# A fused recurrence and maxout MoE on one core: another order of the first loads and of the steps

## The chip, the cores and the metric

The kernel runs on one core of a Trainium2 chip. A core has five engines that work side by side, each through its own queue and in order: TensorE (PE, with its weight loads listed as PEld), VectorE (DVE), ScalarE (ACT), GpSimd (POOL) and SyncE (SP), which here issues all the DMA transfers. An instruction that waits holds up everything behind it on its engine. The metric is the time of one execution in microseconds (us).

## The reference

Two steps follow one another. The first is a gated linear recurrence over time for 4 batches of 8 heads with 768 steps and head size 48; the second takes its outputs, laid out as 3072 tokens of 384 numbers, through a feed-forward layer that keeps the larger of two projections.

```python
for t in range(S):
    state = alpha[:, :, t, :, None] * state + np.einsum('bhd,bhe->bhde', k[:, :, t], v[:, :, t])
    y[:, :, t] = np.einsum('bhd,bhde->bhe', q[:, :, t], state)
...
h1 = x @ w1
h2 = x @ w2
g = np.maximum(h1, h2)
return (g @ w_out)
```

All inputs and the output are float32.

## The kernel before

The work is cut into 12 units (u = 0 to 11). Unit u is a stretch of 256 time steps of one batch: the batch is u mod 4 and the stretch is u div 4, so that units 0 to 3 begin the four batches and unit u takes its state from unit u − 4. A unit has two chunks (cc) of 128 steps.

The recurrence of a unit is done in chunks. `ln` takes the logarithm of alpha on ACT (tile lg). `sums` makes running sums of it on PE with constant masks (tile cs, and the chunk decays dps in a corner of the first cs). `expm`, `expp` and `expd` make exp(−cs) in Em, exp(cs) in place, and the decays de, all on ACT. `kmul` forms kn = k·Em on POOL, `qmul` forms qn = q·exp(cs) on VectorE. `turn` transposes both on PE (tile tp) and copies them out on VectorE (qk). `kvmm` multiplies kn by v for the state, `kvsum` takes that out of PSUM on VectorE (tm) and `state` scales it on POOL (sb). `pmm` forms the products of k and q on PE (pp) and `pmask` masks them on VectorE (pt). `ystate` and `yin` add up the output y from the state and from the masked products (ya), and ACT casts it (xn). `xturn` transposes it (xp), and VectorE copies that to xt, the input of the MoE.

The MoE uses max(h1, h2) = relu(h1 − h2) + h2. So it needs w1 − w2 (`wsub`, VectorE, in four quarters, tile w12), and w2·w_out (tile w2o), which PE forms once: `wturn` transposes w2, `wcast` casts w_out to 16 bits in two halves on ACT and POOL, `wmul` multiplies in two halves, `wout` copies the result out on ACT. `hid(u, f2)` makes one of four hidden pairs, six matmuls and a ReLU (on ACT, or on VectorE for the fourth pair unless told otherwise; tile gT). `outp(u, n)` makes one of the two output blocks: three matmuls of xt with w2o, eight of gT with w_out; ACT copies the block to outs and SP stores it. `vcast` casts v on POOL and ACT. `dummies` issues matmuls on zeros (tile warm) whose results nobody reads.

PSUM has eight banks. They are handed out under three tags: "m" with two banks in turn (hidden pairs, outputs, w2 transposes, dummies), "pp" with two (the products; in the beginning two parts of w2·w_out), and "g" with four in turn (cs, tp, kv, ya, xp, and one part of w2·w_out).

The order on every engine is the order in which the program calls these steps (a manual schedule, lines 465 to 617): a hand-written start for units 0 to 2, then a loop in which iteration u does the state and the y of unit u, the sums, exponentials and turns of unit u + 1, and the MoE of unit u − 1. The loads have four buffers for each input; iteration u issues the loads of unit u + 4. The loads before the loop stand on SP in the order of lines 113 to 122: all of unit 0, w2, w_out, w1, all of unit 1.

Of the kernel before, what the change touches and what calls it, by code (L numbers as in the profile page):

```python
# [15 lines left out]
def kernel(  # L16
# [27 lines left out]
    nc = tc.nc  # L44
# [162 lines left out]

    def sums(u):
        X = st[u]
        lg = X["lg"]  # L210
        cs = [new("g", [128, 512], FP32, 4, "cs") for _ in range(2)]
        X["csv"] = csv = [x[:, 0 : H * D].rearrange("p (h d) -> p h d", h=H) for x in cs]
        X["dps"] = dps = cs[0][:, H * D : H * D + 4 * HP].rearrange("p (j b n) -> p j b n", j=HP, b=2)
        for hp in range(HP):
            for j in range(2):
                nc.tensor.matmul(
                    dps[:, hp], lhsT=pair(lg[:, j], hp), rhs=halves, start=(j == 0), stop=(j == 1)
                )
        for j in range(2):
# [159 lines left out]
    def xturn(u):  # L379
        X = st[u]  # L380
        xp = new("g", [128, ND, 2, C], FP16, 4, "xp")
        for cc in range(2):
# [24 lines left out]

    def outp(u, n):
        X = st[u]
        d, b = divmod(u, B)  # L410
        if n == 0:
            X["outs"] = mp.tile([128, 2, DM], FP32, tag="outs", bufs=2, name="outs")
        op = new("m", [128, DM], FP32, 2, "op")
        for ds in range(ND):
            nc.tensor.matmul(op, lhsT=X["xt"][:, ds, n, :], rhs=w2o[:, ds, :], start=(ds == 0), stop=False)  # L415
        for f in range(NF):
# [19 lines left out]
    def wmul(n):  # L436

        if n == 0:
            wqs.extend([new("pp", [128, DM], FP32, 2, "wq") for _ in range(2)] + [new("g", [128, DM], FP32, 4, "wq")])
        for ds in range(ND):  # L440
# [54 lines left out]
    kvsum(0, 1)  # L495
    ystate(0)
    dummies(2)
    wturn(1)
    yin(0)
    wturn(2)  # L500
    wcast(0)
    dummies(2)
    xturn(0)
    ln(1)
    dummies(4)
    wmul(0)
    wcast(1)
    wsub(0)
    wsub(1)
    wsub(2)  # L510
    wsub(3)
    wmul(1)
    sums(1)
    wout()

    load(3)
    hid(0, 0, False)
    expm(1, 0)
    expp(1, 0)
    hid(0, 1, True)  # L520
    kmul(1, 0)
    qmul(1, 0)
    expm(1, 1)
    expp(1, 1)
    hid(0, 2, False)
    expd(1)
    kmul(1, 1)
    qmul(1, 1)
    vcast(1)
    hid(0, 3, True)  # L530
    load(4)
    turn(1, 0)
    turn(1, 1)
    outp(0, 0)
    kvmm(1, 0)
    pmm(1, 0)
    kvmm(1, 1)
    kvsum(1, 0)
    state(1, 1)
    pmask(1, 0)  # L540
    kvsum(1, 1)
    ln(2)
    dummies(3)
    pmm(1, 1)
    pmask(1, 1)
    ystate(1)
    outp(0, 1)
    yin(1)
    sums(2)
    exps(2)  # L550
    dummies(3)
    xturn(1)
    for cc in range(2):
        kmul(2, cc)
    state(2, 0)
    vcast(2)
    for cc in range(2):
        qmul(2, cc)
    dummies(2)
    hid(1, 0)  # L560
    hid(1, 1)
    turn(2, 0)
    hid(1, 2)
    turn(2, 1)
    hid(1, 3)
    load(5)


    for u in range(2, NU):
# [8 lines left out]
        if more(u):  # L578
            kvmm(u, 1)
        if nxt:  # L580
            ln(u + 1)
        if u > 2:
            hid(u - 1, 0)
            hid(u - 1, 1)
        else:
            outp(1, 0)
        if nxt:
# [10 lines left out]
        if u > 2:  # L598
            hid(u - 1, 2)
            hid(u - 1, 3)  # L600
        if nxt:
            for cc in range(2):
                qmul(u + 1, cc)
        yin(u)
# [42 lines left out]
```

## Time and profile before

| what | value |
|---|---|
| median of 11 runs | 157.35 us (156.52 to 158.69) |
| the profiled execution's own time | 156.48 us |
| its span, first to last instruction | 154.8 us |
| mean granted TensorE clock | 0.978 |
| PE busy | 140.4 us, 91% |
| VectorE busy | 93.8 us, 61% |
| ACT busy | 91.4 us, 59% |
| POOL busy | 56.3 us, 36% |
| read from and written to HBM | 23.59 MB and 4.72 MB |

The profile is one execution. Busy time is the time in which an engine ran an instruction; a wait is idle time and is put down to the event that ended it. The dummies count as busy (35 of them, 11.8 us), so a busy PE is not always useful. A stage view gives the busy times in a stretch of the span and the share of its clock that PE was granted there. The chain of waits is followed back from the last instruction. A DMA row gives the issue on SP; its landing comes later by the time that the DMA view lists.

### The profile page before, as it was taken

The page shows a single profiled execution, that of the slowest core. Times are in us where ns is not written, and L with a number is a line of the kernel's source. Part 1 is how long each engine was busy: PE and PEld are TensorE (multiplying, and loading weights), DVE is VectorE, ACT ScalarE, POOL GpSimd, SP SyncE. Part 2 cuts the span into 40 slices and gives each one's busy share as a digit, 9 for nine tenths or more (in the row PEclk, how much of TensorE's full clock was granted, in tenths as well). Part 3 has the DMA queues.
Part 4 walks back from the last instruction along what each step waited for, and adds up shares of the span by engine and source line. Part 5 has one row for each costly group of instructions (what it writes and reads, how often), then busy time and mean ns, then how long its engine had stood idle before and what let it go on. Part 6 is the DMA issues. An engine that isn't in the chain of part 4 may idle for free.

```text
span 154.8 us, 4245 instructions
## 1 busy us (share of the span) xinstructions
PE 140.4 (91%) x1683; PEld 101.5 (66%) x1683; DVE 93.8 (61%) x191; ACT 91.4 (59%) x188; POOL 56.3 (36%) x111
## 2 busy tenths in 40 slices
PE   6965993998999898999999999999999999999991
PEld 2334751574677586777787777887778778767760
DVE  5058772085558778676687784957757577664110
ACT  3475405473393778486694884966938579445421
POOL 7391400064081626219055171371632805410000
PEclk9999699599999999999999999999999999999999
DMA  4999999999699897988969899797896902020202
GB/s 121 267 388 374 357 300 238 204 171 227 108 246 139 226 229 128 235 131 235 204 115 309 121 248 209 128 319 111 197 263 113 309 16 89 4 102 4 95 6 102
DMA packets 76339, 28.58 MB, mean 185 GB/s; under 512 B 71712, under 2 KB 74528, under 8 KB 76320
## 3 DMA queue, kind: packets, MB, share of 16 engines
q1 hardware_dynamic: 76320, 28.32, 79.3%
q8 instruction: 13, 0.21, 0.7%
q14 instruction: 6, 0.05, 0.1%
HBM read 23.59 MB, written 4.72 MB: 183 GB/s over the span
## 4 chain that ended last, share of the span: by engine, by line
PE 68%; SPq 8%; DMA 7%; DVE 6%; ACT 5%; issue 4%; POOL 1%; ACTq 0%; DVEq 0%
PE op L417 20%; PE hp L399 16%; PE op L415 8%; DMA af<-in_alpha_dram 7%; PE tp L285 6%; SPq L121 4%; PE pp L334 3%; PE cs L226 3%; DVE pt L340 3%; SPq L75 2%; PE xp L386 2%; PE wq L442 2%; PE ya L370 2%; PE kv L307 2%; ACT cs L241 2%
## 5 line engine op out<-in xcount | busy, mean ns | idle before, releaser
L274 POOL TENSOR_TENSOR kn<-kf,Em 128x384 f16<-128x384 f32 x24 | 23.5, 997 | 35.2 <-ACT Em L236 35.2
L399 PE MATMUL hp<-xt,w 128*128 128x256 f16 x288 | 35.8, 273 | 0.3 <-DVE xt L388 0.2
L417 PE MATMUL op<-wo,gT 128*128 128x384 f16 x192 | 35.1, 326 | 0.0
L340 DVE TENSOR_TENSOR pt<-pp,um 128x512 f16<-128x512 f32 x48 | 30.9, 686 | 3.1 <-PE pp L334 2.4
L420 ACT COPY outs<-op 128x384 f32<-128x384 f32 x24 | 11.5, 478 | 35.4 <-PE op L417 24.3
L399 PEld LDWEIGHTS <-w 128*128 128x128 f16 x288 | 26.8, 98 | 5.2 <-issue 1.3
L417 PEld LDWEIGHTS <-gT 128*128 128x128 f16 x192 | 18.8, 98 | 12.4
L266 POOL TENSOR_TENSOR sb<-tm,dd 128x192 f16<-128x192 f32 x20 | 10.1, 506 | 42.4 <-DVE tm L320 31.2
L404 ACT ACTIVATE gT<-hp 128x512 f16<-128x512 f32 x35 | 20.8, 598 | 4.9 <-PE hp L399 3.9
L292 DVE COPY qk<-tp 128x1024 f16<-128x1024 f16 x20 | 13.7, 687 | 11.6 <-PE tp L285 11.6
L406 DVE TENSOR_SCALAR gT<-hp 128x512 f16<-128x512 f32 x13 | 9.0, 692 | 15.4 <-PE hp L399 15.4
L320 DVE TENSOR_TENSOR tm<-kv,sb 64x192 f32<-64x192 f32 x32 | 11.3, 352 | 8.7 <-PE kv L307 8.4
L415 PE MATMUL op<-w2o,xt 128*128 128x384 f16 x72 | 15.6, 325 | 0.4
L278 DVE TENSOR_TENSOR qn<-qf,cs 128x384 f16<-128x384 f32 x24 | 12.3, 547 | 5.6 <-ACT de L246 5.6
L190 ACT ACTIVATE lg<-af 128x768 f16<-128x768 f32 x12 | 10.1, 844 | 7.8 <-DMA af<-in_alpha_dram 7.5
L236 ACT ACTIVATE Em<-cs 128x384 f32<-128x384 f32 x24 | 11.7, 490 | 2.7 <-PE cs L226 2.1
L377 ACT CAST xn<-ya 128x384 f16<-128x384 f32 x24 | 10.4, 491 | 4.8 <-PE ya L370 4.4
L463 PE MATMUL warm<-wz 128*128 128x512 f16 x35 | 11.8, 460 | 1.3 <-DVE halves L146 1.3
L204 ACT CAST v<-vf 64x384 f16<-64x384 f32 x24 | 12.2, 510 | 1.2 <-DMA vf<-in_v_dram 0.6
L202 POOL CAST v<-vf 64x384 f16<-64x384 f32 x24 | 12.0, 501 | 0.7
L334 PE MATMUL pp<-qk 48*128 48x128 f16 x192 | 10.4, 217 | 1.6 <-DVE pt L340 1.2
L241 ACT ACTIVATE cs<-cs 128x384 f32<-128x384 f32 x24 | 11.8, 493 | 0.0
(60 smaller groups left out, 167.2 us busy)
## 6 DMA issues: line engine op xcount, KB each, us to landing
af<-in_alpha_dram SPq DMA_DIRECT2D x12, 384.0 KB, 6.1
vf<-in_v_dram SPq DMA_DIRECT2D x12, 384.0 KB, 4.5
out_dram<-outs SPq DMA_DIRECT2D x11, 384.0 KB, 4.7
kf<-in_k_dram SPq DMA_DIRECT2D x40, 96.0 KB, 4.5
qf<-in_q_dram SPq DMA_DIRECT2D x40, 96.0 KB, 4.0
w2f<-in_moe_w_dram SPq DMA_DIRECT2D x3, 512.0 KB, 5.9
wof<-in_moe_w_out_dram SPq DMA_DIRECT2D x2, 768.0 KB, 9.0
w1f<-in_moe_w_dram SPq DMA_DIRECT2D x4, 384.0 KB, 10.3
```

Source lines behind the costliest of these rows:

```text
L202: nc.gpsimd.tensor_copy(out=o, in_=i)
L204: nc.scalar.copy(out=o, in_=i)
L241: nc.scalar.activation(out=X["csv"][cc], in_=X["csv"][cc], func=ACTF.Exp)
L274: nc.gpsimd.tensor_mul(out=X["kn"][cc][:, :, 0:D], in0=part(u, "kf", cc), in1=X["Em"][cc])
L278: nc.vector.tensor_mul(out=X["qn"][cc][:, :, 0:D], in0=part(u, "qf", cc), in1=X["csv"][cc])
L292: nc.vector.tensor_copy(out=X["qk"][:, cc], in_=tp.rearrange("p n h t -> p (n h) t"))
L334: nc.tensor.matmul(pa[a][:, j, :], lhsT=qk[r, 1, j, :], rhs=qk[r, 0, j, :], start=True, stop=True)
L340: nc.vector.tensor_mul(out=pt[:, a], in0=X["pa", cc][a], in1=um.unsqueeze(1).to_broadcast([128, HP, C]))
L399: nc.tensor.matmul(hp[:, n, :], lhsT=w12[:, ds, f * 128 : (f + 1) * 128], rhs=X["xt"][:, ds].rearrange("p n t -> p (n t)"), start=(ds == 0 ...
L404: nc.scalar.activation(out=gT[:, 2 * f2 : 2 * f2 + 2, :], in_=hp, func=ACTF.Relu)
L415: nc.tensor.matmul(op, lhsT=X["xt"][:, ds, n, :], rhs=w2o[:, ds, :], start=(ds == 0), stop=False)
L417: nc.tensor.matmul(op, lhsT=X["gT"][:, f, n * C : (n + 1) * C], rhs=wo16[:, f, :], start=False, stop=(f == NF - 1))
```

## The change

It has four parts.

- The first loads stand in another order: alpha, k and q of unit 1 come between w2 and w_out, w1 is last of the weights, and v of unit 1 follows it.
- In the start, the steps of unit 1 up to its masks (logarithm, sums, exponentials, products, turns, pair products) are called ahead of MoE 0 and partly ahead of the end of unit 0; what is left of unit 1 and the start of unit 2 follow between and behind the outputs of MoE 0. The two parts of w2·w_out that used the "pp" banks use the "m" banks.
- The four banks in turn, "g", become four banks with fixed uses, g0 to g3: cs and tp on g0 and g1, ya and kv on g2 and g3, xp on g2, the third part of w2·w_out on g3. Outs has four buffers instead of two.
- In the loop, the sums are split in two calls (`sumd`, `sumc`) and the output in two (`outx`, the three matmuls with w2o, and `outg`, the eight with w_out). Three hidden pairs instead of two stand ahead of the exponentials of the next unit, the fourth goes to ACT between them, the first output is called ahead of `yin`, both turns ahead of `xturn`, and the logarithm is taken one unit earlier, at the end of the iteration.

```diff
@@ the loads
         nc.sync.dma_start(out=w2f[:, ds], in_=moe_w2[ds * 128 : (ds + 1) * 128])
+    load_a(1)
+    load_fat(1, "kf", k)
+    load_fat(1, "qf", q)
...
         nc.sync.dma_start(out=w1f[:, :, f], in_=moe_w1.rearrange("(s p) f -> p s f", p=128)[:, :, f])
-    load(1)
+    load_v(1)
@@ banks and buffers
-        cs = [new("g", [128, 512], FP32, 4, "cs") for _ in range(2)]
+        cs = [new(f"g{i}", [128, 512], FP32, 1, "cs") for i in range(2)]
-        tp = new("g", [128, 2, HP, C], FP16, 4, "tp")
+        tp = new(f"g{cc}", [128, 2, HP, C], FP16, 1, "tp")
-        X["kvp", cc] = kvp = new("g", [128, HP, 2 * D], FP32, 4, "kv")
+        X["kvp", cc] = kvp = new(f"g{3 - cc}", [128, HP, 2 * D], FP32, 1, "kv")
-        X["ya"] = ya = [new("g", [128, 2, HP, D], FP32, 4, "ya") for _ in range(2)]
+        X["ya"] = ya = [new(f"g{2 + a}", [128, 2, HP, D], FP32, 1, "ya") for a in range(2)]
-            X["outs"] = mp.tile([128, 2, DM], FP32, tag="outs", bufs=2, name="outs")
+            X["outs"] = mp.tile([128, 2, DM], FP32, tag="outs", bufs=4, name="outs")
@@ the start, behind the first state sums
     kvsum(0, 1)
+    dummies(2)
+    wturn(1)
+    ln(1)
+    dummies(2)
+    sums(1)
     ystate(0)
-    dummies(2)
-    wturn(1)
+    exps(1)
     yin(0)
+    kmul(1, 0)
+    kmul(1, 1)
     wturn(2)
+    dummies(2)
+    qmul(1, 0)
+    qmul(1, 1)
+    xturn(0)
+    turn(1, 0)
+    dummies(2)
+    turn(1, 1)
     wcast(0)
...
+    pmm(1, 0)
+    pmask(1, 0)
     wmul(0)
     wcast(1)
     wsub(0)
+    pmm(1, 1)
+    pmask(1, 1)
+    wmul(1)
+    wout()
+
+    load(3)
+    hid(0, 0, True)
     wsub(1)
+    hid(0, 1, True)
     wsub(2)
...
@@ the loop
         if u > 2:
             hid(u - 1, 0)
             hid(u - 1, 1)
+            if nxt:
+                sumd(u + 1)
+            hid(u - 1, 2)
...
         if nxt:
-            sums(u + 1)
-            exps(u + 1)
-            for cc in range(2):
-                kmul(u + 1, cc)
-            state(u + 1, 0)
+            sumc(u + 1)
+            expm(u + 1, 0)
+            expp(u + 1, 0)
+            expm(u + 1, 1)
         if more(u):
             kvsum(u, 1)
         pmm(u, 1)
         ystate(u)
         pmask(u, 1)
         if u > 2:
-            hid(u - 1, 2)
-            hid(u - 1, 3)
+            hid(u - 1, 3, True)
         if nxt:
+            expp(u + 1, 1)
+            expd(u + 1)
...
+        outp(u - 1, 0 if u > 2 else 1)
         yin(u)
-        outp(u - 1, 0 if u > 2 else 1)
         if nxt:
             turn(u + 1, 0)
+            turn(u + 1, 1)
+        if u > 2:
+            outx(u - 1, 1)
         xturn(u)
         if nxt:
-            turn(u + 1, 1)
             vcast(u + 1)
+        if u + 2 < NU:
+            ln(u + 2)
         if u > 2:
-            outp(u - 1, 1)
+            outg(u - 1, 1)
```

How this moves the instructions is shown at three places. The first is SP's queue from w2 on, before (af, kf, qf and vf are alpha, k, q and v; wof and w1f the weights w_out and w1):

```order
L115 DMA w2f<-in_moe_w_dram 128x1024 x3
L118 DMA wof<-in_moe_w_out_dram 128x4x384 x2
L121 DMA w1f<-in_moe_w_dram 128x3x256 x4
L75 DMA af<-in_alpha_dram 128x8x96
L75 DMA kf<-in_k_dram 128x8x96
L75 DMA qf<-in_q_dram 128x8x96
L75 DMA vf<-in_v_dram 128x8x96
```

and now:

```order
L115 DMA w2f<-in_moe_w_dram 128x1024 x3
L75 DMA af<-in_alpha_dram 128x8x96
L75 DMA kf<-in_k_dram 128x8x96
L75 DMA qf<-in_q_dram 128x8x96
L121 DMA wof<-in_moe_w_out_dram 128x4x384 x2
L124 DMA w1f<-in_moe_w_dram 128x3x256 x4
L75 DMA vf<-in_v_dram 128x8x96
```

Three loads of unit 1 went ahead of six transfers of weights; v of unit 1 stays last.

The second is ACT in the start, from the cast of w2 on, before (lg is the logarithm of alpha, wo the cast w_out, w2o the product w2·w_out):

```order
L482 CAST w2h<-w2f 128x1024 x3
L377 CAST xn<-ya 128x8x48 x2
L452 CAST wo_163<-wof 128x768
L190 ACTIVATE lg_124<-af 128x16x48
L452 CAST wo_163<-wof 128x768
L449 CAST w2o<-wq 128x384 x3
L236 ACTIVATE Em<-cs 128x384
L241 ACTIVATE cs<-cs 128x384
L404 ACTIVATE gT<-hp 128x512
```

and now:

```order
L501 CAST w2h<-w2f 128x1024 x3
L193 ACTIVATE lg_124<-af 128x16x48
L247 ACTIVATE Em<-cs 128x384
L252 ACTIVATE cs<-cs 128x384
L247 ACTIVATE Em<-cs 128x384
L252 ACTIVATE cs<-cs 128x384
L257 ACTIVATE de<-cs 128x16
L388 CAST xn<-ya 128x8x48 x2
L471 CAST wo_163<-wof 128x768 x2
L468 CAST w2o<-wq 128x384 x3
L415 ACTIVATE gT<-hp 128x512 x3
```

The logarithm and the exponentials of unit 1 went ahead of the y of unit 0 and of both casts of w_out.

The third is ACT in one iteration of the loop (u = 4), from the logarithm on, before:

```order
L190 ACTIVATE lg_126<-af 128x16x48
L404 ACTIVATE gT<-hp 128x512 x2
L236 ACTIVATE Em<-cs 128x384
L241 ACTIVATE cs<-cs 128x384
L236 ACTIVATE Em<-cs 128x384
L241 ACTIVATE cs<-cs 128x384
L246 ACTIVATE de<-cs 128x16
L404 ACTIVATE gT<-hp 128x512
L377 CAST xn<-ya 128x8x48 x2
L420 COPY outs<-op 128x384
L204 CAST v_1382<-vf 64x384 x2
L420 COPY outs<-op 128x384
```

and now, from the logarithm that closes iteration 3:

```order
L193 ACTIVATE lg_126<-af 128x16x48
L439 COPY outs<-op 128x384
L415 ACTIVATE gT<-hp 128x512 x3
L247 ACTIVATE Em<-cs 128x384
L252 ACTIVATE cs<-cs 128x384
L247 ACTIVATE Em<-cs 128x384
L415 ACTIVATE gT<-hp 128x512
L252 ACTIVATE cs<-cs 128x384
L257 ACTIVATE de<-cs 128x16
L439 COPY outs<-op 128x384
L388 CAST xn<-ya 128x8x48 x2
L207 CAST v_1386<-vf 64x384 x2
```

Three ReLUs stand ahead of the exponentials instead of two, the fourth, which was VectorE's, stands between them, and the first output copy stands ahead of the cast of y.

More of the change, by code (lines that the diff above doesn't have):

```diff
@@ L380, in xturn @@
         X = st[u]
-        xp = new("g", [128, ND, 2, C], FP16, 4, "xp")
+        xp = new("g2", [128, ND, 2, C], FP16, 1, "xp")
         for cc in range(2):
@@ L408, in outp, with outx, outg @@
     def outp(u, n):
+        outx(u, n)
+        outg(u, n)
+    def outx(u, n):
+        X = st[u]
+        if n == 0:
+            X["outs"] = mp.tile([128, 2, DM], FP32, tag="outs", bufs=4, name="outs")
+        X["op"] = op = new("m", [128, DM], FP32, 2, "op")
+        for ds in range(ND):
+            nc.tensor.matmul(op, lhsT=X["xt"][:, ds, n, :], rhs=w2o[:, ds, :], start=(ds == 0), stop=False)
+    def outg(u, n):
         X = st[u]
         d, b = divmod(u, B)
-        if n == 0:
-            X["outs"] = mp.tile([128, 2, DM], FP32, tag="outs", bufs=2, name="outs")
-        op = new("m", [128, DM], FP32, 2, "op")
-        for ds in range(ND):
-            nc.tensor.matmul(op, lhsT=X["xt"][:, ds, n, :], rhs=w2o[:, ds, :], start=(ds == 0), stop=False)
+        op = X["op"]
         for f in range(NF):
@@ L438, in wmul @@
         if n == 0:
-            wqs.extend([new("pp", [128, DM], FP32, 2, "wq") for _ in range(2)] + [new("g", [128, DM], FP32, 4, "wq")])
+            wqs.extend([new("m", [128, DM], FP32, 2, "wq") for _ in range(2)] + [new("g3", [128, DM], FP32, 1, "wq")])
         for ds in range(ND):
@@ L508 @@
     wsub(0)
-    wsub(1)
-    wsub(2)
-    wsub(3)
+    pmm(1, 1)
+    pmask(1, 1)
     wmul(1)
-    sums(1)
     wout()
     load(3)
-    hid(0, 0, False)
-    expm(1, 0)
-    expp(1, 0)
+    hid(0, 0, True)
+    wsub(1)
     hid(0, 1, True)
[L521 to L528, printed above, removed]
+    wsub(2)
+    dummies(2)
+    hid(0, 2, True)
+    wsub(3)
+    dummies(2)
     vcast(1)
@@ L531 @@
     load(4)
-    turn(1, 0)
-    turn(1, 1)
+    ln(2)
     outp(0, 0)
     kvmm(1, 0)
-    pmm(1, 0)
     kvmm(1, 1)
@@ L539 @@
     state(1, 1)
-    pmask(1, 0)
     kvsum(1, 1)
[L542 to L548, printed above, removed]
     sums(2)
     exps(2)
-    dummies(3)
-    xturn(1)
+    outp(0, 1)
     for cc in range(2):
         kmul(2, cc)
-    state(2, 0)
-    vcast(2)
     for cc in range(2):
         qmul(2, cc)
-    dummies(2)
-    hid(1, 0)
-    hid(1, 1)
+    ystate(1)
+    yin(1)
     turn(2, 0)
-    hid(1, 2)
     turn(2, 1)
-    hid(1, 3)
+    dummies(1)
+    xturn(1)
+    dummies(1)
+    vcast(2)
+    for f2 in range(4):
+        hid(1, f2)
+    ln(3)
     load(5)
@@ L579 @@
             kvmm(u, 1)
-        if nxt:
-            ln(u + 1)
         if u > 2:
```

14 lines of the change are left out of this document (10 added, 4 removed).

## The prediction

> **What bounds the kernel now.** I read first the busy times by stage, with the cuts at the points where a unit's first k-v product starts (47.48 us is unit 2, 55.59 unit 3, 66.09 unit 4, 106.27 unit 8, 135.90 unit 11). The columns are the stage, its length, and each engine's busy time; after POOL come the granted TensorE clock, the DMA share and GB/s.
>
> ```profile
> 13.97:25.83 11.86, 7.47 (x73) 5.08 (x68) 8.40 (x14) 3.20 (x6) 2.10 (x3) 0.86 1.12 314
> 25.83:30.21 4.38, 4.38 (x24) 2.30 (x24) 0.00 (x0) 1.51 (x4) 0.00 (x0) 0.61 1.05 221
> 30.21:47.48 17.27, 16.11 (x185) 11.76 (x184) 10.26 (x19) 10.86 (x25) 7.75 (x13) 1.00 1.03 186
> 47.48:55.59 8.11, 7.54 (x106) 5.40 (x104) 6.34 (x14) 4.57 (x12) 3.60 (x6) 1.00 0.88 207
> 55.59:66.09 10.50, 10.04 (x132) 7.60 (x130) 8.31 (x17) 7.24 (x15) 4.28 (x8) 1.00 1.03 180
> 66.09:106.27 40.18, 39.91 (x545) 31.10 (x544) 29.10 (x56) 28.46 (x60) 17.11 (x32) 1.00 0.94 200
> 106.27:135.90 29.63, 29.20 (x398) 22.70 (x396) 19.98 (x36) 20.75 (x45) 12.84 (x24) 1.00 0.55 135
> 135.90:154.80 18.90, 15.16 (x152) 10.52 (x149) 5.23 (x9) 6.83 (x13) 0.51 (x1) 1.00 0.16 63
> ```
>
> From unit 4 on PE is busy 39.91 of 40.18 us: there the order of PE's work is the bound and only a few tenths per unit are to be had. Before 30 us it is another kernel: VectorE does nothing from 25.83 to 30.21, and PE works there at 0.61 of its clock. The chain of waits says why.
>
> ```profile
> 13.97 10.23 DMA af<-in_alpha_dram
> 24.22 0.84 ACT lg L190
> 25.06 0.73 ACT wo L452
> 25.83 3.09 PE wq L442 x12
> ```
>
> ACT stands with the logarithm of unit 1 at the head of its queue until alpha of unit 1, loaded behind all the weights, lands at 24.2. Behind it wait the last cast of w_out, the second half of w2·w_out, and so MoE 0. What unit 1 needs has no other work to hide behind until 30 us.
>
> **The loads.** Total bytes up to v of unit 1 stay the same; the order changes. Two landings are read from the timeline (the wait in brackets ends with them), one from an issue and its time to landing.
>
> ```profile
> 12.97 1.04 ACT L482 CAST w2h<-w2f 128x1024 f16<-128x1024 f32 x1 [0.24 <-DMA w2f<-in_moe_w_dram]
> ...
> 17.24 0.83 POOL L453 CAST wo<-wof 128x768 f16<-128x768 f32 x1 [0.85 <-DMA wof<-in_moe_w_out_dram]
> ```
> ```profile
> 22.43 1.33 SPq L75 DMA_DIRECT2D vf<-in_v_dram  x1
> ```
> ```profile
> vf<-in_v_dram SPq DMA_DIRECT2D x1, 384.0 KB, 6.0
> ```
>
> w2 is in at 13.0, w_out at 17.2, alpha 1 at 24.2, v 1 at 22.4 + 6.0 = 28.4. So k, q and v of unit 1 take (28.4 − 24.2)/3 = 1.4 us each, and w_out (17.2 − 13.0) = 4.2. In the new order alpha 1 lands at about 14.4, k at 15.8, q at 17.2, w_out at 21.4, the last quarter of w1 1.4 before v, at 27.0, and v again at 28.4. Everything from unit 2 on lands as before. Moved past on SP's queue: six weight transfers go behind three loads; w_out is 4.2 later and w1 too. The gain of 9.8 us on alpha 1 is paid by those 4.2.
>
> **The head, step by step.** Durations of one instruction, from the groups by line (VectorE, then ACT; the mean in ns stands after the comma):
>
> ```profile
> L340 DVE TENSOR_TENSOR pt<-pp,um 128x512 f16<-128x512 f32 x48 | 30.9, 686 | 3.1 <-PE pp L334 2.4
> L292 DVE COPY qk<-tp 128x1024 f16<-128x1024 f16 x20 | 13.7, 687 | 11.6 <-PE tp L285 11.6
> L278 DVE TENSOR_TENSOR qn<-qf,cs 128x384 f16<-128x384 f32 x24 | 12.3, 547 | 5.6 <-ACT de L246 5.6
> ...
> L457 DVE TENSOR_TENSOR w<-w1f,w2f 128x768 f16<-128x768 f32 x4 | 3.6, 954 | 0.0
> ```
> ```profile
> L404 ACT ACTIVATE gT<-hp 128x512 f16<-128x512 f32 x35 | 20.8, 598 | 4.9 <-PE hp L399 3.9
> L204 ACT CAST v<-vf 64x384 f16<-64x384 f32 x24 | 12.2, 510 | 1.2 <-DMA vf<-in_v_dram 0.6
> ```
>
> Logarithm and sums of unit 1 now run at 14.5 to 16.5, beside transfers that were waited for anyway. VectorE becomes the bound of the stretch. It takes up the new order behind the second state sum of unit 0:
>
> ```profile
> 16.21 0.71 DVE L320 TENSOR_TENSOR tm<-kv,sb 64x192 f32<-64x192 f32 x2
> ```
>
> From 16.9 it has two w2 copies, two q products, the x copy, two transposed copies, four masks and four w1 − w2 quarters: eight at 0.69, three at 0.55, four at 0.95, together 11.0. With about 1.1 lost to PE's third w2 turn, to the turns of unit 1 and to its pair products, the last quarter is done at 29.0; w1 (27.0) is in time. The fourth hidden pair of MoE 0 then takes PE 0.65 (six matmuls; twelve stand for 1.32 below, 99.70 to 101.02); its ReLU waits on ACT behind the third ReLU and the two casts of v (0.6 and 1.0) and ends near 31.8. Logarithm of unit 2 to 32.65, sums 33.4, second output 35.3 (1.95 by the rows below, 101.47 to 103.42), the two y parts 36.0, x of unit 1 cast by 37.1 and turned by 37.9. Its copy stands behind two transposed copies of unit 2 on VectorE, to 38.95; MoE 1's four hidden pairs, 2.6 us, end at 41.7. There unit 2's first product stood at 47.48 before: **5.8 us**. Bounds: 4.2 if every wait of the sum is half a microsecond longer three times over, 6.6 if PE's clock and VectorE's 1.1 both come out better.
>
> **Later units.** PE rows of a middle unit (7), its VectorE row, and PE and ACT rows of a late one (10):
>
> ```profile
> 99.15 0.62 PE L358 MATMUL ya<-sb,qk 48*128 48x48 f16 x16
> 99.70 1.48 PE L399 MATMUL hp<-xt,w 128*128 128x256 f16 x12
> 101.02 0.56 PE L370 MATMUL ya<-v,pt 128*128 128x48 f16 x16
> 101.47 0.65 PE L415 MATMUL op<-w2o,xt 128*128 128x384 f16 x3
> 101.96 1.46 PE L417 MATMUL op<-wo,gT 128*128 128x384 f16 x8
> ```
> ```profile
> 98.63 0.71 DVE L320 TENSOR_TENSOR tm<-kv,sb 64x192 f32<-64x192 f32 x2
> ```
> ```profile
> 130.40 0.56 PE L370 MATMUL ya<-v,pt 128*128 128x48 f16 x16
> 131.10 0.65 PE L415 MATMUL op<-w2o,xt 128*128 128x384 f16 x3
> ```
> ```profile
> 130.44 0.61 ACT L404 ACTIVATE gT<-hp 128x512 f16<-128x512 f32 x1
> ```
> ```profile
> 138.44 0.38 PE L334 MATMUL pp<-qk 48*128 48x128 f16 x7 [0.30 <-DVE pt L340]
> ```
>
> In the middle unit y's state part reaches PE at 99.15, but the sum that frees its bank ends at 98.63 + 0.71 = 99.34: 0.2 lost. The third hidden pair (0.65) now stands ahead of it: 0.2 back in each of units 4 to 7, **0.8**. In the late unit the output starts 0.70 after the y part, in the middle one 0.45: it waits for the ReLU that frees its bank, which stands behind all the exponentials and ends at 131.05. The new order puts that ReLU before them: 0.25 in each of units 8 to 10, **0.7**. In the last unit the third pair fills a wait of 0.30 and the piece before it: **0.5**. Unit 2's stage has 0.57 idle and unit 3's 0.46, mostly waits for masks, and the second output and the third pair now lie there: **0.6** and **0.4**. Together 3.0. Bounds: −1.5 (each of nine units gains a wait of 0.17, which no row excludes) to 3.0. The fourth ReLU on ACT (0.6 for VectorE's 0.69) costs nothing while ACT, near 7.1 of 10 us busy, is ahead of PE; by my sum q's second product is ready 0.45 before PE turns it and x's cast 0.25 before its turn. These are thin covers, so I count 2.5 of the 3.0. Four output buffers and the fixed PSUM banks cost nothing by themselves; the banks drop the wait of the second turn for the x cast.
>
> Sum: 5.8 + 2.5 = 8.3. The profiled execution took 156.48 with a span of 154.8, so 148.2 of its own kind; the median of the runs, 157.35, stands 0.87 above it, which gives **149.0 us**.
>
> **The clock.** For the new head the window of the clock matters; the rows first.
>
> ```profile
> 13.15:16.56 3.41, 1.87 (x39) 1.33 (x39) 3.35 (x7) 0.87 (x1) 1.27 (x2) 1.00 1.06 370
> 16.56:19.98 3.42, 3.42 (x40) 2.87 (x38) 1.75 (x3) 1.59 (x3) 0.83 (x1) 0.50 1.10 354
> ```
>
> A window with PE busy 1.87 of 3.41 was followed by one at half clock; the next, full and made largely of transposes, was followed by full clock again (the first row above has 0.86 over both). I expect about 2.4 us busy in each window of the new head, and no half clock. The Trainium skill, "TensorE: Matmul & The Clock Gate", Part 4: PE-mode transpose, says that transposes do not count as PE-busy in the same way. By that rule the trace agrees only in part, since the full window of transposes did restore the clock.
>
> **The rivals.**
> *A half-clock window stays.* The new head has sixteen k-q turns, six x turns and eight w2 turns between 17 and 22 us and little else. If they don't hold the clock, one window of 3.4 us stretches PE's work by up to 1.7; VectorE hides part, 1.3 remains: 150.3. This is what the rule of the Trainium skill named above would make of it.
> *The loads become the bound.* Rows for unit 4's alpha: issue, time to landing, use.
>
> ```profile
> 41.41 0.51 SPq L75 DMA_DIRECT2D af<-in_alpha_dram  x1
> ```
> ```profile
> af<-in_alpha_dram SPq DMA_DIRECT2D x1, 384.0 KB, 6.0
> ```
> ```profile
> 56.10 0.84 ACT L190 ACTIVATE lg<-af 128x768 f16<-128x768 f32 x1
> ```
>
> It lands at 47.4 and is used 8.7 later. The logarithm moves 1.4 forward within the stages, and unit 3 starts 6.4 earlier: 0.9 of cover is left. DMA is near 0.94 to 1.03 busy until 106 us, so it can hardly run faster. If the stream comes 4 us later relative to PE, ACT blocks on it and 3 us are lost: 152.0. For it: the thin 0.9. Against: every transfer from unit 2 on keeps its place.
> *The late w1 decides.* If w_out and w1 land 2 us later than I set them, the last w1 − w2 quarter ends at 31 and all behind it shifts: 151.0.
> *Slower.* ACT, with the fourth ReLU between the exponentials, delivers q's scale late in every unit; decay, q products and the turns on PE follow. It decides once it is 0.45 late. At 1.5 late, units 3 to 11 lose 1.05 each: 9.5 against a gain of 8.3, so 158.5. Against: ACT's 7.1 of 10 us.
> *The head doesn't move* (the sums of unit 1 stay tied to something else), and the small waits cancel the rest: 157.3. The order on each queue is written by hand, and the transfer of alpha 1 was what ended the wait, so little speaks for it.
>
> **How the numbers follow.** Forecast 0.58, with its own range 147.0 to 151.0; half clock 0.10; loads 0.16; late w1 0.08; unmoved 0.03; slower 0.05. The range 146.5 to 153.0 takes in all but the last two and some 0.1 at the edges of the others. A measurement of this kernel tells about 0.5% from no change: faster by more 0.92, within 0.03, slower 0.05.
>
> **What would show it.** The logarithm of unit 1 near 14.5 us with almost no DMA wait; VectorE without a gap between 20 and 29; unit 2's first product at 41 to 43; the fourth pair of a middle unit following y's state part 0.2 sooner than the 0.55 of 99.15 to 99.70; ACT's logarithm with no wait for alpha from unit 4 on. I am wrong if unit 2 starts after 44.5, if PE idles at the turns of each unit, or if ACT's waits for alpha exceed 2 us behind 40 us.

## The result and the profile after

| | before | after |
|---|---|---|
| median of the runs | 156.94 us (156.35 to 158.69, 47 runs) | 148.3 us (148.0 to 148.83, 12 runs) |
| span of the profiled execution | 154.8 us | 146.5 us |
| mean granted TensorE clock | 0.978 | 0.998 |

The ratio is 0.9437, with a 95% interval of 0.9414 to 0.9461. Predicted were 149.0 us, with a range of 146.5 to 153.0. The runs of before are more here than in the prediction, since they were repeated beside each kernel; their median is 0.4 lower. Of the kernels below, loads_only and no_dummies were profiled in an execution slower than most of their others (159.48 us against a median of 156.89, and 151.11 against 147.46), so their spans stand above their medians.

The page of the changed kernel: busy times of the engines, the granted clock in 40 slices, and the shares of the chain that ended last.

```profile
PE 135.9 (93%) x1681; PEld 97.1 (66%) x1681; DVE 87.3 (60%) x180; ACT 97.3 (66%) x199; POOL 56.5 (39%) x111
PEclk9999999999999999999999999999999999999999
PE 83%; DVE 8%; ACT 3%; DMA 3%; issue 1%; DVEq 0%
```

PE is busy 4.5 us less than before (140.4), mostly because the two windows of 3.4 us at half clock, in which it was busy throughout, are gone (half clock stands only in the last half microsecond, where PE has nothing to do). ACT is busier by 5.9, mostly by the fourth ReLU, which VectorE has given up.

The same stages as in the prediction, cut again where a unit's first k-v product starts (41.90 us is unit 2, then 49.56, 59.53, 98.58 for unit 8 and 127.36 for unit 11). Columns: stage, length, busy time of PE, weight loads, VectorE, ACT and POOL, granted clock, DMA share, GB/s.

```profile
13.97:26.74 12.77, 10.98 (x130) 6.88 (x129) 11.05 (x21) 5.93 (x12) 4.11 (x5) 1.00 1.14 329
26.74:41.90 15.16, 14.38 (x153) 10.05 (x150) 6.47 (x12) 10.90 (x23) 5.87 (x11) 1.00 0.95 177
41.90:49.56 7.66, 7.54 (x107) 5.26 (x104) 6.51 (x13) 5.01 (x13) 3.61 (x6) 1.00 1.02 185
49.56:59.53 9.97, 9.73 (x129) 7.45 (x130) 7.43 (x15) 8.35 (x17) 4.28 (x8) 1.00 0.89 197
59.53:98.58 39.05, 39.05 (x546) 30.11 (x545) 27.00 (x52) 30.03 (x64) 17.10 (x32) 1.00 0.97 199
98.58:127.36 28.78, 28.78 (x397) 22.08 (x396) 18.40 (x33) 21.68 (x47) 12.84 (x24) 1.00 0.84 198
127.36:146.50 19.14, 15.26 (x152) 10.36 (x149) 4.54 (x8) 7.33 (x14) 0.51 (x1) 0.99 0.16 63
```

In the first row PE is busy 10.98 of 12.77 us and VectorE 11.05, at full clock. VectorE still has a stretch without work, but a later one: 4.26 us from 29.02 on, until a product of PE comes at 33.28. From unit 4 to unit 10 the profile shows no idle time of PE at all (39.05 of 39.05, 28.78 of 28.78). Stage by stage against the prediction:

| term | predicted gain | measured, from the stage rows |
|---|---|---|
| start, up to unit 2 | 5.8 | 47.48 − 41.90 = 5.58 |
| unit 2's stage | 0.6 | 8.11 − 7.66 = 0.45 |
| unit 3's stage | 0.4 | 10.50 − 9.97 = 0.53 |
| units 4 to 7 | 0.8 | 40.18 − 39.05 = 1.13 |
| units 8 to 10 | 0.7 | 29.63 − 28.78 = 0.85 |
| last unit | 0.5 | 18.90 − 19.14 = −0.24 |
| sum | 8.8, counted 8.3 | 8.30 |

The logarithm of unit 1 in the timeline of the changed kernel, and VectorE's last quarters of w1 − w2:

```profile
14.41 0.84 ACT L193 ACTIVATE lg<-af 128x768 f16<-128x768 f32 x1 [0.44 <-DMA af<-in_alpha_dram]
...
26.33 2.69 DVE L476 TENSOR_TENSOR w<-w1f,w2f 128x768 f16<-128x768 f32 x3
```

Alpha of unit 1 ends a wait of 0.44 us at 14.41 where it ended one of 10.23 at 24.2. VectorE's last quarter ends at 26.33 + 2.69 = 29.02, where the prediction has 29.0.

### The profile page after: what moved, and what is told of

Same layout as the page of the kernel before. It is cut to its first block, busy times and chain, and to the rows that moved or that the text cites. A ratio compares the mean times of both kernels' runs of the same rounds, so it can differ in the third digit from the quotient of the medians.

```text
span 146.5 us, 4239 instructions
## 1 busy us (share of the span) xinstructions
PE 135.9 (93%) x1681; PEld 97.1 (66%) x1681; DVE 87.3 (60%) x180; ACT 97.3 (66%) x199; POOL 56.5 (39%) x111
## 4 chain that ended last, share of the span: by engine, by line
PE 83%; DVE 8%; ACT 3%; DMA 3%; issue 1%; DVEq 0%
PE hp L410 23%; PE op L436 21%; PE op L429 8%; PE tp L296 7%; PE pp L345 4%; PE cs L237 3%; PE ya L381 3%; PE wq L461 3%; DMA af<-in_alpha_dram 3%; PE kv L318 2%; PE xp L397 2%; DVE pt L351 2%; DVE qk L303 2%; PE ya L369 2%; PE cs L223 2%; DVE qk L301 1%
## 5 line engine op out<-in xcount | busy, mean ns | idle before, releaser
L410 PE MATMUL hp<-xt,w 128*128 128x256 f16 x288 | 37.2, 273 | 0.8 <-DVE xt L399 0.6
L415 ACT ACTIVATE gT<-hp 128x512 f16<-128x512 f32 x46 | 27.4, 596 | 14.4 <-PE hp L410 13.7
L410 PEld LDWEIGHTS <-w 128*128 128x128 f16 x288 | 26.1, 97 | 6.1 <-issue 2.2
L429 PE MATMUL op<-w2o,xt 128*128 128x384 f16 x72 | 15.6, 326 | 0.0
L303 DVE COPY qk<-tp 128x1024 f16<-128x1024 f16 x20 | 12.9, 686 | 4.3 <-PE tp L296 4.3
L247 ACT ACTIVATE Em<-cs 128x384 f32<-128x384 f32 x24 | 11.6, 485 | 3.6 <-PE cs L237 3.6
L207 ACT CAST v<-vf 64x384 f16<-64x384 f32 x24 | 12.2, 510 | 1.2 <-DMA vf<-in_v_dram 0.7
L482 PE MATMUL warm<-wz 128*128 128x512 f16 x33 | 11.2, 448 | 1.3 <-DVE halves L149 1.3
L296 PE MATMUL tp<-ident,kn 128*128 128x128 f16 x96 | 9.2, 218 | 2.2 <-DVE qn L289 2.2
L345 PE MATMUL pp<-qk 48*128 48x128 f16 x192 | 9.7, 217 | 1.2 <-DVE qk L301 1.1
```

Of the source, the lines that this page charges most:

```text
L207: nc.scalar.copy(out=o, in_=i)
L296: nc.tensor.transpose(tp[:, n, j, :], pair(src, j), ident)
L303: nc.vector.tensor_copy(out=X["qk"][:, cc], in_=tp.rearrange("p n h t -> p (n h) t"))
L345: nc.tensor.matmul(pa[a][:, j, :], lhsT=qk[r, 1, j, :], rhs=qk[r, 0, j, :], start=True, stop=True)
L410: nc.tensor.matmul(hp[:, n, :], lhsT=w12[:, ds, f * 128 : (f + 1) * 128], rhs=X["xt"][:, ds].rearrange("p n t -> p (n t)"), start=(ds == 0 ...
L415: nc.scalar.activation(out=gT[:, 2 * f2 : 2 * f2 + 2, :], in_=hp, func=ACTF.Relu)
```

## Experiments

Each kernel is told by two numbers of its profiled execution: where the first pair product of unit 2 starts (the start ends there) and the time from there to the end of the span. Before and after have these rows:

```profile
47.75 0.40 PE L334 MATMUL pp<-qk 48*128 48x128 f16 x8
```
```profile
42.16 0.40 PE L345 MATMUL pp<-qk 48*128 48x128 f16 x8
```

| kernel | unit 2's first pair product | from there to the end | span | median | ratio to before, 95% |
|---|---|---|---|---|---|
| before | 47.75 | 107.05 | 154.8 | 156.94 | |
| after | 42.16 | 104.34 | 146.5 | 148.3 | 0.9414 to 0.9461 |
| head_only | 42.40 | 107.10 | 149.5 | 151.26 | 0.9617 to 0.9667 |
| loop_only | 46.98 | 104.42 | 151.4 | 153.11 | 0.9726 to 0.9782 |
| loads_only | 44.90 | 112.90 | 157.8 | 156.89 | 0.9930 to 0.9997 |
| loads_outs4 | 45.03 | 107.07 | 152.1 | 153.71 | 0.9762 to 0.9847 |
| old_loads | 53.26 | 104.34 | 157.6 | 158.61 | 1.0087 to 1.0155 |
| before_outs4 | 47.85 | 107.05 | 154.9 | 156.57 | 0.9957 to 1.0014 |
| outs2 | 42.04 | 114.06 | 156.1 | 158.09 | 1.0041 to 1.0117 |
| no_loads | 41.91 | 104.39 | 146.3 | 148.45 | 0.9401 to 0.9520 |
| v_twice | 43.23 | 115.97 | 159.2 | 160.46 | 1.0148 to 1.0287 |
| pair_back | 42.55 | 107.95 | 150.5 | 151.71 | 0.9634 to 0.9702 |
| no_dummies | 44.99 | 104.41 | 149.4 | 147.46 | 0.9337 to 0.9470 |
| trimmed | 40.97 | 103.93 | 144.9 | 146.85 | 0.9315 to 0.9389 |

### Start and loop apart

head_only is the changed kernel with the loop of before (the edit against the changed kernel, cut to its main lines):

```diff
-    ln(3)
@@ the loop, as before
+        if nxt:
+            ln(u + 1)
...
-            hid(u - 1, 3, True)
+            hid(u - 1, 2)
+            hid(u - 1, 3)
```

> The changed kernel with the loop as it was before (third pair, fourth ReLU, turns, logarithm and output in the old places); loads, start, banks and four output buffers stay changed. My theory: the start and the loop are worth separate amounts, 5.6 us and 2.7 us by the two traces, so this run stands at about 148.3 + 2.7 = 151.0. Rival: the head start alone runs into the loads or into the stores, and most of it is given back in the loop: 153 or more.

loop_only is the other half: loop, banks and output buffers of the change, start and loads of before (the edit against the kernel before, cut to its main lines):

```diff
+    ln(3)
@@ the loop, as changed
+            hid(u - 1, 2)
...
-            hid(u - 1, 2)
-            hid(u - 1, 3)
+            hid(u - 1, 3, True)
```

> The changed loop, banks and four output buffers behind the start and the order of loads of before. My theory: the loop alone gives its 2.7 us, 156.9 - 2.7 = 154.2. Rival: the loop's gain comes only with the earlier start: 156.5.

The two halves hardly touch each other. With the new start unit 2 begins at 42.2 to 42.4 whichever loop follows, and with the old loop the rest takes 107.1 whichever start precedes; with the new loop it takes 104.3 to 104.4. So the new start is worth 47.75 − 42.40 = 5.35 and the new loop 107.05 − 104.42 = 2.63, by the traces. By the medians, each against the runs of before beside it (156.69), head_only gains 5.4 and loop_only 3.6, together 9.0 where the change gains 8.6. The 0.4 too much fits the traces: loop_only also has unit 2 at 46.98 instead of 47.75, in a head that it leaves nearly unchanged. Its two half-clock windows follow each other (15.6 to 22.4 us) where those of before stand at 16.6 and 26.8; whether that alone is the 0.8 was not tried. The fixed PSUM banks were not tried alone either: both halves have them.

### New loads, old order, and the output buffers

loads_only is the kernel before with the new order of loads alone:

```diff
         nc.sync.dma_start(out=w2f[:, ds], in_=moe_w2[ds * 128 : (ds + 1) * 128])
+    load_a(1)
+    load_fat(1, "kf", k)
+    load_fat(1, "qf", q)
...
-    load(1)
+    load_v(1)
```

> The kernel before with the new order of loads and nothing else. My theory: alpha of unit 1 is there at 14.4 us but its logarithm stands behind the casts of y and w_out, and w_out comes 4.2 us later; MoE 0 gets ready about 1.5 to 2 us sooner, since the second half of w2 w_out no longer waits for alpha: 155.2. Rival: the order of loads is the whole start: 151.5. Other rival: the late weights make it slower: 158.

old_loads is the changed kernel with the old order of loads (the same lines the other way round).

> The changed kernel with the loads in the old order (alpha, k, q of unit 1 behind all weights). My theory: ACT then waits for alpha to 24.2 us with the exponentials and all that follows behind it, nearly all of the start is 9.3 us later, and the time goes back to about 157.5. Rival: the order of steps is what counts, VectorE's work catches up: 151.

With the new loads alone unit 2 begins 2.85 earlier, half of the 5.6; with the new steps alone it begins 5.5 later than before, because ACT, in order, now stands at the logarithm of unit 1 ahead of all of MoE 0. The row of old_loads:

```profile
24.49 0.84 ACT L190 ACTIVATE lg<-af 128x768 f16<-128x768 f32 x1 [10.51 <-DMA af<-in_alpha_dram]
```

So the start's gain belongs to neither part; it needs both. But loads_only showed something that no step of the prediction had: its 2.85 at unit 2 were gone by unit 5 (first pair products at 63.50 for unit 4 and 77.92 for unit 5, 14.4 apart where before has 10.05), and the median was 156.89. The reason stands in the timeline:

```profile
76.58 0.48 ACT L423 COPY outs<-op 128x384 f32<-128x384 f32 x1 [7.19 <-DMA out_dram<-outs]
```

ACT waits 7.2 us to copy an output block into one of the two buffers, because the store that empties it hasn't landed. The median of 156.89 shows the same loss. That gave a new theory: stores stand on SP behind the loads, and compute that comes earlier only waits longer for them. Then the four buffers carry the gain. outs2 is the changed kernel with two:

```diff
-            X["outs"] = mp.tile([128, 2, DM], FP32, tag="outs", bufs=4, name="outs")
+            X["outs"] = mp.tile([128, 2, DM], FP32, tag="outs", bufs=2, name="outs")
```

> The changed kernel with two output buffers instead of four. The prediction held that the buffers by themselves cost and bring nothing: 148.3. Rival, from the trace after: the store of unit 1 stands on SP behind the loads and lands at 75.6 us, while unit 3 wants its buffer at 66 us; with two buffers ACT stops there for up to 9.5 us, PE with it, and most of the gain of the start is lost: 154 to 157.

It took 158.09, slightly slower than before, with unit 2 at 42.04 as in the changed kernel. The wait is in unit 4; the copy with its wait, and the ten microseconds around it:

```profile
73.93 0.48 ACT L439 COPY outs<-op 128x384 f32<-128x384 f32 x1 [8.66 <-DMA out_dram<-outs]
```
```profile
70.00:80.00 10.00, 4.77 (x34) 3.05 (x35) 1.47 (x4) 3.58 (x7) 0.09 (x1) 0.66 1.03 207
```

The buffer held unit 1's output. Its second block was copied into it long before, but SP issues the store only behind the loads of units 5 and 6 (rows of outs2):

```profile
47.60 0.48 ACT L439 COPY outs<-op 128x384 f32<-128x384 f32 x1 [0.63 <-PE op L436]
```
```profile
69.06 0.52 SPq L445 DMA_DIRECT2D out_dram<-outs  x1
```

The store stands 21 us in SP's queue (48.1 to 69.1) and takes another 4.8 to land. From 50.2 to 69.1 SP is at the issues of those loads for 17.5 us. The same copy in the kernel before:

```profile
74.39 0.48 ACT L420 COPY outs<-op 128x384 f32<-128x384 f32 x1 [2.15 <-DMA out_dram<-outs]
```

The buffer comes free at 74.39 in before, 76.58 in loads_only and 73.93 in outs2, with the store issued at 69.3, 70.6 and 69.1: no earlier by more than half a microsecond, while unit 2 came 2.9 and 5.7 us earlier. In outs2 the idle PE also falls to a mean clock of 0.66 (the row of 70.00 to 80.00), so the work that follows the wait is slow as well.

Whether four buffers are worth anything by themselves, and whether they bring back the lost 2.85 of loads_only, two kernels with the same one-line edit (`bufs=2` to `bufs=4`) tell: before_outs4 and loads_outs4.

> The kernel before with four output buffers instead of two and nothing else. Theory: before, ACT stops for stores too (5.4 us in three waits), but PE is not held up by it, since the units come later; the buffers bring nothing alone: 156.7, within 0.5. Rival: the waits did cost PE: 155.5 or less.

> The kernel before with the new order of loads and four output buffers. With two buffers this order brought unit 2 forward by 2.9 us (pair products at 44.90 instead of 47.75) and lost it again at unit 4, where ACT waited 7.2 us for a store. Theory of the stores: with four buffers the 2.9 us stay, 156.7 - 2.9 = 153.8. Rival: they are lost in another way, to the loads or the loop: 156 or more.

before_outs4 is before, to about 0.1 us in every unit from 2 on; the interval holds 1. loads_outs4 took 153.71, with unit 2 at 45.03 and then 107.07 to the end, and its waits of ACT for a buffer are all for PE's product, none for a store:

```profile
ACT outs L423 <- PE op L420: 35.4, 24, 3.6
```

The theory holds: the buffers gain nothing in the old kernel, and without them the rest gains nothing.

### Are the loads of later units the next bound?

no_loads leaves out the loads of units 4 to 11; they compute on the inputs of units 2 and 3. v_twice loads v a second time into a tile that nobody reads, for unit 0 and for each unit from 2 on (its expectation leaves out unit 0).

```diff
+        if u > 3:
+            st[u] = {n: st[2 + u % 2][n] for n in ("af", "kf", "qf", "vf")}
+            return
```
```diff
+        x = ldp.tile([128, H, 2, D], FP32, tag="vx", bufs=1, name="vx")
+        nc.sync.dma_start(
+            out=x.rearrange("p h j d -> p h (j d)"),
+            in_=rows(v, u, 0, 2 * C).rearrange("h (p j) d -> p h (j d)", j=2),
+        )
```

> The changed kernel in which units 4 to 11 load nothing and compute on the inputs of units 2 and 3 (their results are those of other inputs). My theory: the loads do not bind, PE is busy all of the time from unit 4 on: 148.3, within 0.5. Rival: loads and their traffic hold back PE, ACT or the stores: faster by 1 us or more.

> The changed kernel with one more transfer of 384 KB per unit from unit 2 on (v once more into a tile that nobody reads), about 1.4 us of the transfer stream in each of ten units. If the cover of the loads is as thin as I took it (0.9 us at unit 4; in the trace after 0.4 us at unit 5), the stream binds at once and the whole comes near 148.3 + 14 - 2 = 160. Rival: the cover is still several us, as the 8.7 us before: 152 or less.

Without loads units 4 to 7 take the same 39.05 us as with them, at a DMA share of 0.11 instead of 0.97. The row of no_loads:

```profile
59.28:98.33 39.05, 39.05 (x546) 30.11 (x545) 27.01 (x52) 30.04 (x64) 17.15 (x32) 1.00 0.11 42
```

So they cost this kernel nothing that can be measured (148.45 against 148.3), neither as a bound nor by contention. One more transfer of 384 KB per unit costs 12.2 us (160.46 − 148.3; by the traces 1.1 up to unit 2 and 11.6 behind it), and ACT then waits for alpha in ten units. Two of them, units 0 and 1, wait in the changed kernel too (2.9 us); units 4 to 11 are new, with 17.5:

```profile
ACT lg L198 <- DMA af<-in_alpha_dram: 20.4, 10, 3.8
```

The cover is real but thin. In the changed kernel unit 5's alpha is issued and used here:

```profile
51.06 0.43 SPq L75 DMA_DIRECT2D af<-in_alpha_dram  x1
...
58.65 0.84 ACT L193 ACTIVATE lg<-af 128x768 f16<-128x768 f32 x1
```

The view of transfers lists 7.2 us from issue to landing, so it lands near 58.3, 0.4 us ahead of its use. For unit 4 the same sum gives 2.1 us.

### How near is ACT's chain?

pair_back puts the third hidden pair back behind the state part of y; two ReLUs then stand behind ACT's third exponential.

```diff
-            hid(u - 1, 2)
...
+            hid(u - 1, 2)
             hid(u - 1, 3, True)
```

> The changed kernel with the third hidden pair back behind the y state part in each unit of the loop (its ReLU then stands behind three exponentials). My theory of the loop: PE waits again 0.2 us for the freed bank in units 3 to 7 and about 0.25 us for the later ReLU in units 8 to 10, 148.3 + 1.7 = 150.0. Rival: with the other changes of the loop the place of this pair no longer matters: 148.3.

It took 151.71, 3.4 more than the changed kernel and twice what was expected; a middle unit takes 10.19 us instead of 9.76. PE's rows of unit 4, first in the changed kernel, then in pair_back:

```profile
62.90 0.39 PE L345 MATMUL pp<-qk 48*128 48x128 f16 x8
63.12 0.36 PE L369 MATMUL ya<-sb,qk 48*128 48x48 f16 x16
63.42 0.83 PE L410 MATMUL hp<-xt,w 128*128 128x256 f16 x6
64.09 0.65 PE L429 MATMUL op<-w2o,xt 128*128 128x384 f16 x3
```
```profile
63.06 0.39 PE L345 MATMUL pp<-qk 48*128 48x128 f16 x8
63.54 0.37 PE L369 MATMUL ya<-sb,qk 48*128 48x48 f16 x16
63.84 1.48 PE L410 MATMUL hp<-xt,w 128*128 128x256 f16 x12
65.36 0.65 PE L429 MATMUL op<-w2o,xt 128*128 128x384 f16 x3
```

Both waits that the change took away come back: the state part follows the pair products by 0.48 instead of 0.22 (it waits for VectorE's sum, which starts at 62.77, takes 0.71 and ends at 63.48), and the output follows the twelve hidden matmuls by 1.52 where 1.32 is their pace, since it takes the bank of the third pair and waits for its ReLU. That is 0.26 and 0.20 of the 0.43. The first comes back in units 3 to 8, the second in every unit from 3 on; the expectation had each in some units only. In the changed kernel the four rows follow each other without a gap.

The ReLU is not late because of the exponentials, as the expectation had it. ACT's third exponential and the two ReLUs:

```profile
64.11 0.49 ACT L247 ACTIVATE Em<-cs 128x384 f32<-128x384 f32 x1
64.71 1.25 ACT L415 ACTIVATE gT<-hp 128x512 f16<-128x512 f32 x2
```

The exponential ends at 64.60, the third pair's six matmuls at about 64.67 (63.84 and 0.83 more), and the ReLU starts at 64.71: it waited for PE. The six matmuls of the fourth pair, 0.66 at their pace, are too short to cover it, and the masked y products, which stood between in the kernel before, have moved behind the output. So the run shows what the place of the pair is worth, not how near ACT's chain is. For that the changed kernel's own rows serve: in unit 4 q's second product ends at 66.45, 0.49 ahead of its turn, and the x cast at 67.32, 0.34 ahead of its turn.

### The clock of the start

no_dummies leaves out the fourteen dummies that are issued behind the second state sum of unit 0 (its expectation says twelve).

> The changed kernel without the twelve matmuls on zeros behind the second state sum of unit 0 (about 17 to 38 us). Theory of the clock: PE is busy well under 2.4 of 3.4 us in some window, the granted clock falls to half in the next, and 0.5 to 1.5 us are lost: 149.3, with a clock under 1.00 in the stages from 17 to 32 us. Rival: the clock holds, and PE loses the hold-ups that the dummies cause: 148.0.

In the profiled execution the clock fell at 17.4 and stayed at half for three windows:

```profile
14.00:17.40 3.40, 2.16 (x34) 1.25 (x29) 3.31 (x8) 2.10 (x5) 1.20 (x2) 1.00 1.22 280
17.40:20.80 3.40, 2.71 (x38) 2.31 (x39) 1.96 (x4) 1.36 (x5) 1.26 (x2) 0.51 1.06 373
20.80:24.20 3.40, 2.58 (x25) 2.07 (x25) 2.37 (x5) 1.66 (x2) 1.65 (x2) 0.50 1.10 350
24.20:27.60 3.40, 3.40 (x12) 1.52 (x10) 2.08 (x3) 0.00 (x0) 0.00 (x0) 0.50 1.20 298
27.60:31.00 3.40, 3.40 (x30) 2.16 (x29) 2.68 (x4) 1.44 (x3) 1.62 (x2) 0.98 0.80 144
```

The changed kernel, over the same first two:

```profile
14.00:17.40 3.40, 2.84 (x39) 1.72 (x38) 3.31 (x8) 1.70 (x4) 0.79 (x2) 1.00 1.23 280
17.40:20.80 3.40, 2.97 (x51) 2.12 (x46) 2.77 (x6) 1.65 (x6) 1.67 (x2) 1.00 1.06 374
```

With the dummies PE is busy 2.84 of the 3.40 us ahead, without them 2.16; in the kernel before 1.87 of 3.41 stood ahead of a half-clock window. Unit 2 came at 44.99, and this execution took 151.11 us. Four others, at a clock of 1.00 throughout, took 147.05 to 147.78. So by the medians the dummies cost about 0.8 us when the clock holds without them (the intervals of the two ratios overlap), and 3.6 are lost when it doesn't. That their absence caused the fall is likely but not shown: it came in one execution of five. None of the twelve with dummies was above 148.83; that one had a mean clock of 0.988, which amounts to about one window of 3.4 us at half clock, and lost little by it.

### A faster version

trimmed leaves out six of the fourteen dummies (those beside MoE 0 and the x turn of unit 1), puts the fourth ReLU of MoE 0 ahead of the two casts of v on ACT, and in the last unit lets three matmuls of `outg` go ahead of the x turn.

```diff
-    dummies(2)
...
-    dummies(2)
+    hid(0, 3, True)
     vcast(1)
-    hid(0, 3, True)
...
+        lo = 3 if u == NU - 1 else 0
+        if lo:
+            outg(u - 1, 1, 0, lo)
...
-            outg(u - 1, 1)
+            outg(u - 1, 1, lo)
```

> The changed kernel without the six matmuls on zeros in MoE 0 and around the x turn of unit 1 (the pairs before 22 us stay), the fourth ReLU of MoE 0 ahead of the casts of v on ACT, and in the last unit three matmuls of the output ahead of the x turn, where PE waited 0.45 us. Theory: 0.45 us at the end and 0.3 to 0.6 us at the start, 147.4. Rival: without these matmuls the clock falls to half in some window: 149 or more.

It took 146.85 us (146.44 to 147.31), a ratio of 0.9352 to before and the best of all kernels here. Unit 2 begins 1.2 earlier than in the changed kernel, and the rest is 0.4 shorter. The start keeps its clock (1.00 from 13.15 to 42.00), and the end has three matmuls where there was a wait:

```profile
132.89 0.65 PE L436 MATMUL op<-wo,gT 128*128 128x384 f16 x3
133.50 0.51 PE L397 MATMUL xp<-ident,xn 128*128 128x128 f16 x6
```

How the 1.2 divides between the dummies and the ReLU was not tried; the changed kernel's chain of waits (next section) has the dummies on it and not the ReLU.

## Why the prediction was right, and where it was not

**The bound of the start: right.** ACT at the head of its queue, behind alpha of unit 1, was the cause: old_loads keeps that wait (10.51) and loses everything, and with alpha in front it is 0.44. The gain was 5.58 against 5.8, within the bounds of 4.2 (4.3 by its own three half microseconds) and 6.6.

**What bounds the start now: not VectorE to the end.** VectorE's queue ended at 29.02 as the sum had it, with 1.6 us of waits for 1.1, and two of them, 0.49 for pair products and 0.47 for the first quarter of w1, fall between 20 and 29, where the prediction wanted no gap. But nothing waited for that end. The chain of waits of the changed kernel leaves VectorE at 22.0 and stays on PE until 37:

```profile
24.85 2.06 PE wq L461 x12
26.91 1.31 PE hp L410 x12
28.25 0.61 PE warm L482 x2
28.89 0.81 PE hp L410 x6
29.71 0.45 PE warm L482 x2
30.20 0.82 PE hp L410 x6
```

The last hidden pair, the one that needs the last quarter of w1 − w2, starts at 30.20, 1.18 us behind it. The twenty-four matmuls of w2·w_out (two times 2.06 us) and the dummies, which hold the chain there, are no terms of the sum. That the sum comes out near in spite of this is partly luck: the fourth ReLU ended at 31.89 (31.8 in the sum) because it did wait for the casts of v, but the second output ended at 36.04 for 35.3 and MoE 1's hidden pairs at 42.06 for 41.7.

**The landings: nearly.** The two halves of w_out were set at the latest at 21.4:

```profile
12.80 2.14 SPq L121 DMA_DIRECT2D wof<-in_moe_w_out_dram  x2
...
21.04 0.82 POOL L472 CAST wo<-wof 128x768 f16<-128x768 f32 x1 [1.97 <-DMA wof<-in_moe_w_out_dram]
...
23.15 0.83 POOL L472 CAST wo<-wof 128x768 f16<-128x768 f32 x1 [1.28 <-DMA wof<-in_moe_w_out_dram]
```

The first was in at 21.0, the second only at 23.1, 1.7 late. The prediction counted bytes and left out the issues: SP stood 4.88 us at one of them (the section on the hardware), so that w_out was issued only at 12.80. That this made it late is not shown: the transfers were busy all the while (a DMA share of 1.06 and more in the rows from 14.00 to 20.80 above). The rival in which late weights decide took 2 us of delay to cost 2; here 1.7 on w_out cost nothing that the chain shows, since its second half was cast by 23.98 and PE was at the first half's products until 24.5. Further on, "everything from unit 2 on lands as before" was not exact: unit 4's alpha was issued at 42.97 instead of 41.41 and, by the view of transfers (5.0 us), landed 0.6 later.

**The later units: right in mechanism, small errors in size.** The state part is followed by the hidden pair after 0.30 instead of 0.55, and the output by its own pace. Units 4 to 7 gained 1.13 for 0.8: the wait that the sum costed at 0.2 was 0.25 in each (0.55 − 0.30), and the rest comes from PE's idle time, 0.27 before and none now, which was not in the sum. pair_back, in which both waits come back, shows that they hang on the place of the third pair.

**The last unit: wrong in sign.** The step "In the last unit the third pair fills a wait of 0.30 and the piece before it: 0.5" failed: 0.24 was lost. The wait of 0.30 for the mask did go: the second pair products now follow eighteen hidden matmuls at once. But these take 0.2 longer than their pace (1.48 for twelve, 0.66 for six more), since the third pair waits for the bank that the first pair's ReLU frees; in the other units the running sums stand between. And the first output, now ahead of `yin`, leaves nothing to cover the x cast, which costs 0.45:

```profile
127.95 2.33 PE L410 MATMUL hp<-xt,w 128*128 128x256 f16 x18
130.22 0.40 PE L345 MATMUL pp<-qk 48*128 48x128 f16 x8
...
133.60 0.65 PE L429 MATMUL op<-w2o,xt 128*128 128x384 f16 x3
134.69 0.51 PE L397 MATMUL xp<-ident,xn 128*128 128x128 f16 x6 [0.45 <-ACT xn L388]
```

The prediction followed the hidden pair to the wait it fills, and neither what that pair itself waits for nor the output that moved. The wait for the x cast is the one that trimmed fills.

**The output buffers: a step that was not taken.** "Four output buffers … cost nothing by themselves" is true (before_outs4, and the changed kernel) and beside the point. They decide the result: with two, the same kernel takes 158.09. The row that points there is one of the kernel before, and no step of the prediction uses it:

```profile
ACT outs L420 <- DMA out_dram<-outs: 5.4, 3, 2.2
```

Three waits for stores already stood there, and a start 5.8 us earlier could only lengthen them. A reader of the prediction would have had no reason to expect that a kernel with this head and this loop could be slower than before, and the rival that I set on that side (ACT's exponentials) was another.

**The rivals.** Loads as the bound: the prediction counted 0.9 us of cover left at unit 4; it is 2.1 there, and the least is 0.4, at unit 5. The 3 us of loss did not come, and no_loads leaves no part of it. Half clock: the clock stayed at 1.00 in the traced execution. The rule cited there, from the Trainium skill, "TensorE: Matmul & The Clock Gate", Part 4: PE-mode transpose, that transposes do not count as PE-busy in the same way, would have the turns not hold the clock; the start here, with its dummies, is no test of the turns alone. Nor is the full window that the prediction held against the rule: beside its turns it has 1.06 us of dummies and 0.85 of y products. no_dummies is nearer to a test, and there the clock fell in one execution of five, so it neither bears the rule out nor excludes it. ACT late in every unit: it is not; the covers that the prediction put at 0.45 and 0.25 are 0.49 and 0.34 in unit 4.

**The sum** was 8.3 and the span moved by 8.3, partly because errors cancelled: the last unit was 0.74 worse than set and units 4 to 10 together 0.48 better, the start 0.22 worse, and the 0.5 held back for thin covers took up the rest. So the exact match is luck in part. What separates 149.0 from the measured 148.3 is not the sum but the 0.87 added for the median: the first eleven runs of before had their median that far above the profiled execution, all 47 only 0.46, and the changed kernel 0.03.

## What to carry to other kernels

When loads and stores share one queue in order, a store lands when the loads ahead of it let it; before compute is made earlier, look up which buffers are freed by stores and whether compute would now arrive first. An early load and an early consumer are one change: on in-order engines each alone can be worth half, nothing or less than nothing. When a step is moved up to fill one wait, look up what it had been covering where it stood, above all in the last iteration, which has no next unit to hide it.

## What the runs showed of the hardware

An issue on SP can take long. In the changed kernel the issue for q of unit 1 held SP for 4.88 us, while the transfers ahead were under way:

```profile
7.88 4.88 SPq L75 DMA_DIRECT2D qf<-in_q_dram  x1
```

The five issues ahead of it and the five behind it take 0.4 to 1.4 us each. The kernel before shows it too: its issue for k of unit 1, at 15.49, took 4.17 us. What stands behind such an issue on SP is issued that much later, though the order of bytes is as planned.

The half clock came in steps of about 3.4 us: two single ones in the kernel before, two in a row in loop_only, three in a row in the execution of no_dummies. It ended, in all of these, behind the first window that PE filled: in no_dummies the windows with 2.71 and 2.58 of 3.40 were followed by another at half clock, and the one with 3.40 of 3.40 (24.20 to 27.60) by full clock; in the kernel before one full window (3.42 of 3.42, in the prediction) was enough. And it makes idle time dearer than it looks: the 8.7 us in which outs2 waits for a store are part of ten with a mean clock of 0.66.
